# In the first block of a fused attention, MLP and expert kernel: the second weight step of a round placed ahead of two matmul groups, and ScalarE's order left to the planner

## The chip, the cores and the metric

The kernel runs on one core of a Trainium2 chip. The metric is the device time of one execution in microseconds (us). Five engines matter: TensorE (PE), whose weight loads are listed as PEld; VectorE (DVE); ScalarE (ACT); GpSimd (POOL); and SyncE (SP), which only issues transfers. Each runs its own list of instructions in order and waits on semaphores for the others.

## The reference

Everything is float32 at the interface. A chunked attention over 8 batches, 8 heads, 576 positions and a head size of 64 (chunks of 64 positions) is followed by a two-layer MLP and then by a routed layer of 8 experts with a skip.

```
scores = q_c @ k_c^T / 8 ; attn = softmax(scores) ; x = attn @ v_c   # (4608, 512)
h = x @ w_in                       # (4608, 2048)
x = (h * sigmoid(1.702 h)) @ w_out # (4608, 512)
e = argmax(x @ w_gate) ; p = softmax(x @ w_gate)[e]
out = x + p * relu(x @ w1[e]) @ w2[e]   where x @ w_skip > 0, else x
```

The two matrices of the MLP reach the chip as 64-bit floating-point numbers, as pairs of 32-bit words.

## The kernel before

Each large matmul is made of three matmuls on a faster 32-bit format: an operand is split into a high part (`hi`) and what is left (`lo`), and `hi*hi + hi*lo + lo*hi` is summed. The 4608 rows are worked through in nine blocks of 512 (`j`), each in 16 rounds (`i`), one for each 128 of the 2048 hidden columns. A round of the MLP has these steps:

- `emit_h` (lines 289 to 301): 12 matmuls (H) into one of two PSUM banks `hps`; then ACT makes `sg` (tanh, line 299), and DVE makes `sg` final from it and the bank (line 300), which frees the bank.
- `emit_g` (lines 303 to 310): ACT makes `gh` (line 306), DVE makes `gl` (line 309).
- `emit_y` for the round before (lines 312 to 322): 12 matmuls (Y) into four banks `yps`, the first eight from `gh`, the last four from `gl`.

The attention for the next block is made beside it. In the first block, rounds 1, 4, 7, 10 and 13 have a `burst` (lines 216 to 228): PE makes the scores of one tile of 128 positions and the output of the tile before into the same two banks of tag `at`; DVE reduces and subtracts (lines 168 and 170), ACT takes the exponential (line 175) and copies the output out (line 214). Rounds 3, 6, 9, 12 and 15 have `c0` (DVE lines 178 to 181, the softmax's division) and `c1` (PE transposes line 189, ACT copy line 191). Rounds 0, 3, 6, 9 and 12 have `a` (PE transposes of q and k at line 143, ACT copies at line 145). The transposes use the same two `at` banks.

The first block also turns the 64-bit weights into `hi` and `lo` parts, in 33 steps ("ticks"), one for each of the 32 half matrices and one to drain: 8 are done in the prologue and 25 in block 0. A tick is `tick1` then `tick2` (lines 702 to 717). On half `m` DVE does two bit operations (lines 265 and 266) and POOL one add (line 267). On half `m-1` ACT makes the high part (line 276) and DVE the low part (line 277). For half `m+1` ACT reads the raw words (lines 258 and 259), and for half `m+3` SP issues a load of 512 KB (lines 242 and 247). Rounds 0 to 14 each have one tick (called the first tick here), with its `tick1` set between `gh` and `gl`. The ten rounds 0, 1, 3, 4, 6, 7, 9, 10, 12 and 13 have a second one, issued by the `while` loop at lines 799 and 800.

The order of the instructions on each engine is fixed when the program is built. A planner goes through a modelled time line and gives each engine, whenever it is free, the earliest instruction of the program whose inputs and buffers are ready there. Engines named in `tc.manual_schedule` (line 767, open for the 16 rounds of block 0) keep the order of the program instead. Before the change these are ACT, DVE and POOL; PE and SP are the planner's everywhere, and outside block 0 all engines are.

Of the kernel before, what the change touches and what calls it, by code (L numbers as in the profile page):

```python
# [21 lines left out]
def kernel(  # L22
# [14 lines left out]
    PE, ACT, DVE, POOL, SP = nc.tensor, nc.scalar, nc.vector, nc.gpsimd, nc.sync  # L37
# [43 lines left out]
    def bank(shape, tag, name):  # L81
        return pp.tile(shape, F32, tag=tag, name=name, bufs=PB[tag])
# [206 lines left out]
    def emit_h(i, xh, xl):  # L289
        ps = bank([P, BT], "h", "hps")  # L290
        n = 0
        for kk in range(KD):
            wh = whi[i][:, kk * P:(kk + 1) * P]
            wl = wlo[i][:, kk * P:(kk + 1) * P]
            for a, b in ((wh, xh), (wh, xl), (wl, xh)):
                PE.matmul(ps, a, b[:, kk], start=(n == 0), stop=(n == 3 * KD - 1))  # L296
                n += 1
        sg = mp.tile([P, BT], F32, tag="sg", name="sg", bufs=2)
        ACT.activation(out=sg, in_=ps, func=AF.Tanh, scale=0.851)  # L299
        DVE.scalar_tensor_tensor(sg, sg, 1.0, ps, op0=ALU.add, op1=ALU.mult)  # L300
        return sg

    def emit_g(sg, between=None):
        gh = mp.tile([P, BT], F32R, tag="gh", name="gh", bufs=2)
        gl = mp.tile([P, BT], F32R, tag="gl", name="gl", bufs=2)
        ACT.activation(out=gh, in_=sg, func=AF.Copy, scale=0.5)  # L306
        if between is not None:
            between()
        DVE.scalar_tensor_tensor(gl, sg, 0.5, gh.bitcast(F32), op0=ALU.mult, op1=ALU.subtract)  # L309
        return gh, gl  # L310

    def emit_y(i, g, ys):
        gh, gl = g
        wh, wl = whi[i][:, HW:], wlo[i][:, HW:]
        first, last = i == 0, i == NF - 1
        for t in range(TPB):
            cs = slice(t * P, (t + 1) * P)
            PE.matmul(ys[t], gh[:, cs], wh, start=first, stop=False)  # L318
            PE.matmul(ys[t], gh[:, cs], wl, start=False, stop=False)  # L319
        for t in range(TPB):  # L320
            cs = slice(t * P, (t + 1) * P)
            PE.matmul(ys[t], gl[:, cs], wh, start=False, stop=last)  # L322
# [13 lines left out]
    def gate_load():  # L336
        SP.dma_start(out=wgT[:, :, 0:NE], in_=w_gate.rearrange("(k p) e -> p k e", p=P))

    def gate_rows():
        ps = bank([P, DM], "at", "wgp")  # L340
        for kk in range(KD):
            PE.transpose(ps[0:NE, kk * P:(kk + 1) * P], wgT[:, kk, 0:NE], ident)
        rows = mp.tile([P, DM], F32, tag="x2", name="wgrows", bufs=4)[0:NE]
        ACT.copy(out=rows, in_=ps[0:NE])
        SP.dma_start(out=wgd, in_=rows)
# [171 lines left out]
    def first_row(s):  # L517
        src = emeta[0:1, 1, s:s + 1] if s < NFIRST else meta[0:1, 0, s - NFIRST:s - NFIRST + 1]
        return SP.value_load(src, min_val=0, max_val=NROW - SL)
# [14 lines left out]
    def load_next():  # L534
        if cnt["load"] < len(wq):
            s, n, w = wq[cnt["load"]]
            cnt["load"] += 1
            single = s >= NFIRST + NPAIR and w == 0
            raw2.append((s, n, w, None if single else load_w2(expert(s), n, w)))
# [109 lines left out]
    def new_x1():  # L649
        return [mp.tile([P, 2, BT], F32, tag="x1", name="x1", bufs=2) for _ in range(2)]  # L650
# [43 lines left out]
    tick_n = [0]  # L694

    def tick():


        tick1()
        tick2()  # L700

    def tick1():
        m = tick_n[0]
        if m == 0:
            halves[0].s0()
        if m < 2 * NF:
            halves[m].s1()

    def tick2():
        m = tick_n[0]  # L710
        tick_n[0] += 1
        if 1 <= m <= 2 * NF:
            halves[m - 1].s3()
        if m + 1 < 2 * NF:
            halves[m + 1].s0()
        if m + 3 < 2 * NF:
            halves[m + 3].load()

    def ticks_by(i):

        return min(2 * NF + 1, NTICK0 - (-(2 * NF + 1 - NTICK0) * (i + 1) // (NF - 1)))
# [31 lines left out]
    for j in range(NB):  # L753
        lastb = j + 1 == NB
        if not lastb:
            x1 = new_x1()
        else:
            rs.close()
            rawp = rs.enter_context(tc.tile_pool(name="raw", bufs=2, side="right", reuse_waits="tile"))
            for _ in range(4):  # L760
                load_next()
        ys = [bank([P, DM], "y", "yps") for _ in range(TPB)]
        prev = None
        inorder = ExitStack()
        if j == 0:
            assert tick_n[0] == NTICK0
            inorder.enter_context(tc.manual_schedule(engines={ACT.engine, DVE.engine, POOL.engine}))
        for i in range(NF):
            R = j * NF + i
            nc_ = round_of.get(R - 2)  # L770
            if nc_ is not None and nc_ < NST:
                St[nc_].c0()
            sg = emit_h(i, xh, xl)
            span = NF // 2 - 2 if lastb else NF - 5
            nfill = -(-len(fill) // (span - i)) if i < span else 0
            if nfill:
                fill.pop(0)()
                nfill -= 1
            mid = None
            if j == 0:  # L780
                if i == 7:
                    gate_load()
                elif i == 11:
                    gate_rows()
                if tick_n[0] < ticks_by(i):
                    mid = tick1
            g = emit_g(sg, mid)
            if mid is not None:
                tick2()
            if prev is not None:  # L790
                emit_y(i - 1, prev, ys)
            na = round_of.get(R + 1)
            if na is not None and na < NST:
                St[na].a()
                if na + 1 < NST:
                    St[na + 1].load_qk()
            if nc_ is not None and nc_ < NST:
                St[nc_].c1()
            while j == 0 and tick_n[0] < ticks_by(i):
                tick()  # L800
            kb = round_of.get(R)
            if kb is not None:
                if kb:
                    St[kb - 1].x1 = x1
                burst(St[kb] if kb < NST else None, St[kb - 1] if kb else None)
                if kb < NST:
                    St[kb].load_v()
            for _ in range(nfill):
                fill.pop(0)()
            if late and (i >= span or late[0][0] < j):  # L810
                late.pop(0)[1]()
            if lastb:
                if prev is not None:
                    conv_next2()
                if i == NF // 2:
                    gstack.close()
                    m2 = ctx.enter_context(tc.tile_pool(name="m2", bufs=1, reuse_waits="tile"))
                    for s in range(NEARLY):
                        slots[s].list(first_row(s))
                if i >= NF // 2 + 2 and i - NF // 2 - 2 < NEARLY:  # L820
                    slots[i - NF // 2 - 2].gather((NB - 1) * BT)
            prev = g
        inorder.close()
        if j == 0:
            assert tick_n[0] == 2 * NF + 1
            fstack.close()
            gstack = ExitStack()
            gp = gstack.enter_context(tc.tile_pool(name="gates", bufs=1, reuse_waits="tile"))
            wg = gp.tile([P, NE, DM], F32, name="wg")
            ws = gp.tile([P, DM], F32, name="ws")  # L830
            SP.dma_start(out=ws, in_=w_skip.rearrange("(o d) -> o d", o=1).to_broadcast([P, DM]))
            SP.dma_start(
                out=wg, in_=wgd[0:NE].rearrange("(o e) d -> o e d", o=1).to_broadcast([P, NE, DM]))
        if not lastb:
            xhn = split_x1(x1)
            emit_y(NF - 1, prev, ys)
            xh, xl = xhn
        else:
            slots[0].trans()
            emit_y(NF - 1, prev, ys)  # L840
            conv_next2()
        xs = evac_y(j, ys)
        lg = new_lg()
        if not lastb:
            fill = [lambda t=t, e=e, lg=lg, xs=xs: dot(lg, xs, t, e) for t in range(TPB) for e in range(NE + 1)]
            rt = route(j, lg)
            if j == NB - 3:
                rt.insert(3, order)
            late += [(j + 1, f) for f in rt]
# [108 lines left out]
```

## Time and profile before

| | us |
|---|---|
| median of three runs (lowest to highest) | 1240.87 (1239.23 to 1242.0) |
| the profiled execution | 1239.68 |
| span of its trace | 1237.8 |
| PE busy in the span | 1185.6 (96%) |
| DVE busy | 787.3 (64%) |
| ACT busy | 488.5 (39%) |
| POOL busy | 146.6 (12%) |

The span is what the trace covers. Block 0 lies between about 45 and 175 us of it; before that is the prologue, after it come blocks 1 to 8 and the expert stage. In rows of a timeline, brackets hold the time for which the engine stood idle just before the instruction, and what ended it.

### The profile page before, as it was taken

How to read it: one execution, taken by the hardware profiler on the slowest of the kernel's cores; microseconds unless marked ns; L12 is line 12 of the kernel's file. 1: busy time of each engine (PE TensorE's matmuls, PEld its weight loads, DVE VectorE, ACT ScalarE, POOL GpSimd, SP SyncE). 2: the span in 40 equal slices, each digit the busy share in tenths (PEclk: the TensorE clock that was granted, in tenths of full speed). 3: DMA queues.
4: the chain of work that ended last, by engine and by line, in shares of the span. 5: the costliest groups of instructions: out<-in, count | busy, mean ns of one | idle time of the engine just before them, and what ended most of it. 6: DMA issues, size and time to landing. Idle time of an engine off the chain costs nothing. (4 is left out here: it accounts for less than half of the span.)

```text
span 1237.8 us, 20861 instructions
## 1 busy us (share of the span) xinstructions
PE 1185.6 (96%) x7984; PEld 993.1 (80%) x7984; DVE 787.3 (64%) x1771; ACT 488.5 (39%) x825; POOL 146.6 (12%) x137
## 2 busy tenths in 40 slices
PE   6788899999999999999999999999999999999995
PEld 4666678888888888888888888888788989999985
DVE  5778779349548647746926934954885686666421
ACT  5655643333333324334333333332344444444320
POOL 2332310010010000001001001001021022231110
PEclk9999999999999999999999999999999999999998
DMA  9545441122113113113113112301444667666540
GB/s 217 162 145 145 129 162 43 26 55 87 31 33 104 30 32 95 38 37 99 27 43 100 29 27 54 89 14 38 152 143 130 217 173 259 225 229 219 187 137 8
DMA packets 181846, 128.99 MB, mean 104 GB/s; under 512 B 122335, under 2 KB 155359, under 8 KB 181616
## 3 DMA queue, kind: packets, MB, share of 16 engines
q1 hardware_dynamic: 177072, 117.09, 32.8%
q0 software_dynamic: 4672, 10.54, 2.5%
q8 instruction: 64, 1.05, 0.4%
q14 instruction: 38, 0.31, 0.1%
HBM read 103.59 MB, written 25.04 MB: 104 GB/s over the span
## 5 line engine op out<-in xcount | busy, mean ns | idle before, releaser
L296 PE MATMUL hps<-xh,whi 128*128 128x512 f32 x576 | 232.2, 405 | 9.0 <-DVE sg L300 8.0
L318 PE MATMUL yps<-whi,gh 128*128 128x512 f32 x576 | 228.9, 397 | 4.2 <-ACT gh L306 4.2
L296 PE MATMUL hps<-xl,whi 128*128 128x512 f32 x576 | 227.6, 395 | 0.0
L296 PE MATMUL hps<-xh,wlo 128*128 128x512 f32 x576 | 227.1, 394 | 0.5 <-DVE wlo L277 0.5
L319 PE MATMUL yps<-wlo,gh 128*128 128x512 f32 x576 | 225.7, 392 | 0.0
L300 DVE SCALAR_TENSOR_TENSOR sg<-sg,hps 128x512 f32<-128x512 f32 x144 | 98.5, 684 | 181.6 <-ACT sg L299 180.6
L355 DVE CUSTOM_DVE_ANT_0 junk<-x,wg 128x512 f32<-128x512 f32 x256 | 175.8, 687 | 4.0
L545 DVE TENSOR_TENSOR elo<-rawe,ehi 128x1024 fp32r<-128x1024 f32 x88 | 107.4, 1223 | 84.5 <-ACT ehi L544 79.6
L322 PE MATMUL yps<-whi,gl 128*128 128x512 f32 x576 | 155.4, 391 | 0.0
L299 ACT ACTIVATE sg<-hps 128x512 f32<-128x512 f32 x144 | 85.8, 597 | 165.5 <-PE hps L296 165.3
L544 ACT CAST ehi<-rawe 128x1024 fp32r<-128x1024 f32 x88 | 92.3, 1049 | 139.0 <-PE h2p L610 68.1
L306 ACT ACTIVATE gh<-sg 128x512 fp32r<-128x512 f32 x144 | 91.1, 633 | 129.6 <-DVE sg L300 109.7
L296 PEld LDWEIGHTS hps<-xh,whi 128*128 128x128 f32 x576 | 108.7, 190 | 34.0 <-DVE sg L300 10.6
L318 PEld LDWEIGHTS yps<-whi,gh 128*128 128x128 f32 x576 | 108.7, 189 | 28.3 <-ACT gh L306 5.1
L296 PEld LDWEIGHTS hps<-xh,wlo 128*128 128x128 f32 x576 | 108.9, 189 | 23.7 <-DVE wlo L277 0.9
L319 PEld LDWEIGHTS yps<-wlo,gh 128*128 128x128 f32 x576 | 108.8, 189 | 22.0
L296 PEld LDWEIGHTS hps<-xl,whi 128*128 128x128 f32 x576 | 109.0, 189 | 20.9 <-DVE xl L286 0.6
L322 PEld LDWEIGHTS yps<-whi,gl 128*128 128x128 f32 x576 | 107.6, 188 | 22.3
L408 POOL DMA_INDIRECT tab<-pr,pos x36 | 39.6, 1099 | 674.0 <-DVE st L168 336.0
L309 DVE SCALAR_TENSOR_TENSOR gl<-sg,gh 128x512 fp32r<-128x512 f32 x144 | 99.1, 688 | 30.4 <-ACT gh L306 20.3
L610 PE MATMUL h2p<-xT,ehi 128*128 128x256 f32 x640 | 117.2, 283 | 0.0
L610 PEld LDWEIGHTS h2p<-xT,ehi 128*128 128x128 f32 x640 | 102.0, 191 | 2.6
(172 smaller groups left out, 1522.9 us busy)
## 6 DMA issues: line engine op xcount, KB each, us to landing
rawe<-in_moe_w_dram SPq DMA_DIRECT2D x88, 512.0 KB
v<-in_v_dram SPq DMA_DIRECT2D x144, 64.0 KB
x2d<-x SPq DMA_DIRECT2D x36, 256.0 KB
out_dram<-x SPq DMA_DIRECT2D x36, 256.0 KB
q<-in_q_dram SPq DMA_DIRECT2D x32, 256.0 KB
k<-in_k_dram SPq DMA_DIRECT2D x32, 256.0 KB
raw<-in_moe_w_in_dram SPq DMA_DIRECT2D x16, 512.0 KB
raw<-in_moe_w_out_dram SPq DMA_DIRECT2D x16, 512.0 KB
```

Source lines behind the costliest of these rows:

```text
L296: PE.matmul(ps, a, b[:, kk], start=(n == 0), stop=(n == 3 * KD - 1))
L299: ACT.activation(out=sg, in_=ps, func=AF.Tanh, scale=0.851)
L300: DVE.scalar_tensor_tensor(sg, sg, 1.0, ps, op0=ALU.add, op1=ALU.mult)
L306: ACT.activation(out=gh, in_=sg, func=AF.Copy, scale=0.5)
L309: DVE.scalar_tensor_tensor(gl, sg, 0.5, gh.bitcast(F32), op0=ALU.mult, op1=ALU.subtract)
L318: PE.matmul(ys[t], gh[:, cs], wh, start=first, stop=False)
L319: PE.matmul(ys[t], gh[:, cs], wl, start=False, stop=False)
L322: PE.matmul(ys[t], gl[:, cs], wh, start=False, stop=last)
L355: DVE.tensor_tensor_reduce(junk, xs[t], wg[:, e, :] if e < NE else ws, 1.0, 0.0, ALU.mult, ALU.add, lg[:, t, e:e + 1])
L544: ACT.copy(out=hi, in_=raw)
L545: DVE.tensor_tensor(lo, raw, hi.bitcast(F32), op=ALU.subtract)
L610: PE.matmul(ps[:, f], a[:, c], self.xT[:, b, kk], start=(m == 0), stop=(m == 3 * KD - 1))
```

## The change

Two edits. The loop that issues a round's second tick stood behind `emit_y`, `a` (with the load of the next q and k) and `c1`; it now stands right behind the first tick, ahead of `emit_y`. And ACT is taken out of the set whose order is that of the program in block 0; DVE and POOL stay in it.

```diff
-            inorder.enter_context(tc.manual_schedule(engines={ACT.engine, DVE.engine, POOL.engine}))
+            inorder.enter_context(tc.manual_schedule(engines={DVE.engine, POOL.engine}))
...
             if mid is not None:
                 tick2()
+            while j == 0 and tick_n[0] < ticks_by(i):
+                tick()
             if prev is not None:
                 emit_y(i - 1, prev, ys)
...
             if nc_ is not None and nc_ < NST:
                 St[nc_].c1()
-            while j == 0 and tick_n[0] < ticks_by(i):
-                tick()
             kb = round_of.get(R)
```

## Rows read from the trace of the kernel before

**Rows 1.** By stretch: busy PE, PEld, DVE, ACT, POOL; granted clock, transfer share, GB/s.

```profile
45.00:175.00 130.00, 112.44 (x746) 88.51 (x747) 97.42 (x155) 77.78 (x146) 37.92 (x25) 0.97 0.46 136
175.00:300.00 125.00, 125.00 (x867) 102.40 (x866) 85.42 (x226) 42.49 (x79) 4.21 (x5) 1.00 0.23 64
```

**Rows 2.** Waits of TensorE from 45 to 173 us: total, times, longest.

```profile
PE hps L296 <- DVE sg L300: 6.1, 6, 1.6
PE yps L318 <- ACT gh L306: 4.2, 2, 2.3
PE qTp L143 <- ACT x L214: 3.2, 2, 1.6
PE sv L209 <- ACT qT L191: 2.7, 4, 0.7
PE hps L296 <- ACT xh L285: 1.0, 1, 1.0
PE hps L296 <- DVE wlo L277: 0.5, 1, 0.5
```

**Rows 3.** The same view from 175 us to the end.

```profile
PE xTp L589 <- DMA xg<-x2d,gi: 2.8, 1, 2.8
PE hps L296 <- DVE sg L300: 1.8, 1, 1.8
```

**Rows 4.** Timeline of TensorE, first matmuls behind waits in block 0.

```profile
53.94 0.50 PE L296 MATMUL hps<-xh,whi 128*128 128x512 f32 x1 [0.96 <-DVE sg L300]
...
83.88 0.50 PE L296 MATMUL hps<-xh,whi 128*128 128x512 f32 x1 [1.61 <-DVE sg L300]
...
165.51 0.50 PE L318 MATMUL yps<-whi,gh 128*128 128x512 f32 x1 [1.93 <-ACT gh L306]
```

**Rows 5.** Timeline of ScalarE, rounds 3 to 5.

```profile
80.36 0.58 ACT L191 COPY qT<-pTp 128x512 f32<-128x512 f32 x1 [2.98 <-PE pTp L189]
80.84 0.62 ACT L276 CAST whi<-a 128x512 fp32r<-128x512 f32 x1
81.36 0.70 ACT L258 ACTIVATE r<-raw 128x512 f32<-128x512 f32 x1
...
82.51 0.59 ACT L299 ACTIVATE sg<-hps 128x512 f32<-128x512 f32 x1
...
90.28 0.63 ACT L175 ACTIVATE qT<-qT 128x512 f32<-128x512 f32 x1 [1.84 <-DVE qT L170]
90.81 0.63 ACT L214 COPY x<-sv 128x256 f32<-128x256 f32 x2
```

**Rows 6.** Timeline of VectorE, rounds 1 and 3 to 5.

```profile
58.24 0.68 DVE L277 TENSOR_TENSOR wlo<-a,whi 128x512 fp32r<-128x512 f32 x1
...
81.50 0.69 DVE L277 TENSOR_TENSOR wlo<-a,whi 128x512 fp32r<-128x512 f32 x1 [3.00 <-ACT whi L276]
83.13 0.69 DVE L300 SCALAR_TENSOR_TENSOR sg<-sg,hps 128x512 f32<-128x512 f32 x1 [0.94 <-ACT sg L299]
...
85.41 1.79 DVE L277 TENSOR_TENSOR wlo<-a,whi 128x512 fp32r<-128x512 f32 x1
...
89.44 0.74 DVE L170 TENSOR_TENSOR qT<-sv,st 128x256 f32<-128x256 f32 x2
91.97 0.69 DVE L300 SCALAR_TENSOR_TENSOR sg<-sg,hps 128x512 f32<-128x512 f32 x1 [1.79 <-ACT sg L299]
```

**Rows 7.** Busy time of three rounds (4 to 6), from one line-300 start to another.

```profile
83.13:107.41 24.28, 20.03 (x148) 15.77 (x148) 18.32 (x29) 14.41 (x27) 7.61 (x5) 1.00 0.50 141
```

**Rows 8.** The stretch of block 0 with the lowest granted clock, by engine.

```profile
118.00:121.00 3.00, 3.00 (x9) 2.29 (x9) 2.97 (x4) 1.74 (x4) 1.57 (x1) 0.54 1.10 282
```

**Rows 9.** Timeline of GpSimd, its adds in rounds 1 and 4.

```profile
58.50 1.58 POOL L267 TENSOR_TENSOR a<-a,lf 128x512 uint32<-128x512 uint32 x1 [1.78 <-DVE a L266]
...
85.06 1.59 POOL L267 TENSOR_TENSOR a<-a,lf 128x512 uint32<-128x512 uint32 x1 [5.11 <-ACT whi L276]
```

**Rows 10.** Waits of SyncE's queue from 45 to 173 us, the loads of raw weights.

```profile
SPq L247 <- DVE a L266: 36.6, 11, 10.3
```

## The prediction

> **What bounds the kernel now.** I read the busy times by stretch first. From 175 us on, TensorE is busy in every microsecond of the stretch shown (125.00 of 125.00), and in block 0 only 112.44 of 130.00 [rows 1]. Next its waits. From 175 us to the end there are two, 4.6 us together [rows 3]; in block 0 the six kinds listed come to 6.1 + 4.2 + 3.2 + 2.7 + 1.0 + 0.5 = 17.7 us [rows 2]. So the last block and the expert stage are bound by TensorE, and time taken out of block 0 reaches the end undiminished, because nothing behind it waits for a fixed moment. The change can win little more than these 17.7 us, plus what the clock costs: the granted clock of block 0 is 0.97 over 130 us [rows 1], so 0.03 x 130 = 3.9 us at most, lowest at 0.54 from 118 to 121 us, where TensorE ran almost wholly at the lower level of 1.2 GHz [rows 8].
>
> Then, who is late in block 0? Three rounds take 24.28 us, with TensorE busy 20.03, VectorE 18.32, ScalarE 14.41 and GpSimd 7.61 [rows 7]. None is full. VectorE's list shows why: in that period it stands 3.00 us before the low part of the second tick, 0.94 and 1.79 us before line 300, each time for ScalarE [rows 6]. And ScalarE, which has the most room of the three, was itself standing: 2.98 us before the `c1` copy, for transposes that TensorE had put behind other work, and 1.84 us before the exponential, for VectorE's subtraction [rows 5]. In both places instructions whose inputs had long been there stood behind it in the order of the program: the second tick's line 276 and the next `sg` at 80.84 and 82.51 us, the output copies at 90.81. TensorE feels this two steps later, at 83.88 us for instance [rows 4], because only the finished `sg` frees one of its two `hps` banks.
>
> **The change part by part.** *The moved step.* It issues, for each of ten second ticks, three instructions on ScalarE, three on VectorE, one on GpSimd and mostly one load on SP. It passes `emit_y` (TensorE alone), `a` (TensorE and ScalarE), the loads of q and k (SP) and `c1` (TensorE and ScalarE). No instruction of VectorE or GpSimd is passed, so their lists, which stay in program order, stay as they are. On SP the raw load goes ahead of q and k in the program; that queue stood 36.6 us in eleven waits before raw loads until VectorE's line 266 had freed a buffer [rows 10], so the load leaves when VectorE lets it, a little earlier than now. I put it at 0; it could cost a late q and k, but the waits of TensorE in block 0 show no transfer among them [rows 2], and q and k are fetched a burst ahead. On ScalarE the three instructions leave from behind the two copies of `a` and the `c1` copy. They take 82.51 - 80.84 = 1.67 us [rows 5].
>
> *A wait that the move adds.* The second tick's line 276 needs GpSimd's add of the first tick, 1.58 us [rows 9]. In between ScalarE has the first tick's two reads of raw words, 82.51 - 81.36 = 1.15 us by the same pair [rows 5]. So it may wait some 0.4 us, with two reads and the copies of `a` queued behind. Ten times 0.4 us on an engine that has 24.28 - 14.41 = 9.9 us free in three rounds: 0, and 4 us if all of it were on the path.
>
> *ScalarE's free order.* The planner gives ScalarE the earliest instruction whose inputs are there, so the next `sg` need not stand behind `c1`, nor the output copies and the next `sg` behind the exponential. The trace of before has no such order in block 0; the nearest rows are from 175 to 300 us, where ScalarE is the planner's and TensorE never waits, though with ScalarE at 42.49 of 125 us against 77.78 of 130 [rows 1].
>
> I go through TensorE's waits by place.
> - *Behind `c1`.* The waits on line 300 are 6.1 us in six; 0.96 us is the start of the block, 1.61 us that at 83.88 and another like it a period later. With the larger wait for `gh`, 4.2 - 1.93 = 2.3 us, and the 0.5 us for `wlo` that is 2 x 1.61 + 2.3 + 0.5 = 6.0 us [rows 2, 4]. If `sg` goes ahead of the copy, ScalarE starts it up to 2.98 us earlier, more than any of these: all 6.0 go.
> - *Behind the burst.* The other three waits on line 300, 6.1 - 0.96 - 3.22 = 1.9 us, the wait for `gh` at 165.51, 1.9 us, and the two for the output copies, 3.2 us, make 7.0 us [rows 2, 4]. Line 300 can then follow VectorE's subtraction at once, which saves its 1.79 us wait [rows 6]. But the two `at` banks are also held until the subtractions end, at 89.44 + 0.74 = 90.18 us against 90.81 + 0.63 = 91.44 for the copies [rows 5, 6]: of each 1.6 us wait only 1.26 goes and 0.3 stays, 0.7 together. So 6.3 go.
> - *Kept.* The 0.96 us and 1.0 us at the start, where nothing is reordered, and the four waits for the `c1` copy itself, 2.7 us [rows 2].
>
> That is 12.3 us. Against it: a free ScalarE will often have started a read of raw words just before `sg` or `gh` becomes ready. One takes 0.57 us (half of the 1.15), on average half of it is in the way, and with ten waits in play that is 10 x 0.29 = 2.9 us. What is late next is VectorE's list, which without its 5.7 us of waits needs 18.5 of the 20 us that TensorE needs. The sum is 12.3 - 2.9 = 9.4 us. The profiled execution took 1239.68 us (span 1237.8 and 1.9 around it), so 1230.3; the median shown is 1.2 us above that execution, and I name its equivalent, **1231.5 us**. I take nothing for the clock: rounds 4 to 6 hold waits as long as elsewhere and were granted 1.00 throughout [rows 4, 7], so waits alone do not bring it down, and fewer of them may not hold it.
>
> *A rule weighed.* The low-part subtraction took 1.79 us when it began at 85.41, inside GpSimd's add that had begun at 85.06, and 0.68 us when it began at 58.24, ahead of the add at 58.50 [rows 6, 9]. The Trainium skill, SBUF — State Buffer, "Who interferes with whom", says that a VectorE instruction with two SBUF inputs and a GpSimd one that reads SBUF contend for a port pair and that whichever starts first keeps it throughout; by that rule the trace agrees, and it speaks against the move, which brings the second subtraction back beside an add. By the round-1 row the subtraction comes first and the sum stays; the other outcome is the third rival.
>
> **The rivals.**
> 1. *Only the move acts.* The planner may lay ScalarE's `c1` copy and burst where they were. Then just the 1.67 us ahead of `sg` go: 2 x 1.61 + 1.67 + 0.5 = 5.4 us, 1234.3 in the profile, 1235.5 as a median. For it: the planner's own list for TensorE put the transposes of `c1` late. Against it: `sg`'s matmuls were done long before.
> 2. *All of it.* Copies of `a` made early free the `at` banks, `c1` comes ahead of its need, and with dense work the clock holds: 17.7 - 2.0 + 3.9 = 19.6 us, 1221.3 as a median. Against it: VectorE's 18.5 of 20 us leave little room for jitter.
> 3. *The subtraction comes second.* If the high part is late by 0.3 us in rounds 3, 6, 9 and 12, four subtractions begin inside the add, 4 x (1.79 - 0.69) = 4.4 us, all of it on VectorE's path: 9.4 - 4.4 = 5.0 us gained, 1235.9.
> 4. *Slower: reads of raw words taken first.* Raw words and their buffers are ready early, so the planner's list may put both reads ahead of `sg` or `gh`, and VectorE, whose order is fixed, then stands with line 300 or 309 at the head of its queue, the tick's bit operations and the burst behind it. 1.15 us in each of 16 rounds is 18.4 us against the 12.3 won: 6.1 us slower, 1247.0. It decides from the eleventh such round (12.3 / 1.15 = 10.7). For it: VectorE has only 1.5 us to spare in 20, and the planner's modelled times need not be the chip's. Against it: `sg` and `gh` come earlier in the program than the reads that compete.
>
> **How the numbers follow.** Forecast 0.34, only the move 0.14, all of it 0.13, the subtraction 0.07: faster by over 0.2% 0.68. Waits that come back elsewhere to within 0.2% (2.5 us, about what a measurement of this kernel can tell from no change): 0.08. Slower 0.24. The likeliest case's own range is 1227 to 1236, its gain half lost or half as large again. The range runs from the second rival, 1221, to just past the fourth, 1248; about 0.08 lies outside at the top and 0.04 below.
>
> **What would show it.** Right: the lists of VectorE and GpSimd unchanged in block 0; VectorE's 3.00 us wait before line 277 and its 1.79 us before line 300 gone; `sg` on ScalarE ahead of the `c1` copy and of the exponential; TensorE's waits in block 0 near 9 us; three rounds in about 22 us. The first rival shows as a `c1` copy still followed by `sg`; the third as second subtractions of 1.79 us in rounds 3, 6, 9 and 12; the fourth as line 258 and 259 directly ahead of `sg` or `gh`, with VectorE waiting for ScalarE over 1 us in most rounds. The prediction is wrong if block 0 is not shorter, or if what it wins is lost behind 175 us.

## The result, and the profile after

The changed kernel takes 1230.54 us (four runs, 1228.8 to 1230.99) against 1241.02 for the kernel before: a ratio of 0.9913, 95% interval 0.9901 to 0.9925, 10.5 us less. The forecast was 1231.5. The span fell from 1237.8 to 1227.1 us. The terms of the sum were forecast less well than its size.

Busy time by stretch (columns as in [rows 1]), with two stretches of three rounds, 4 to 6 and 7 to 9, from one start of line 300 to another, that answer to [rows 7]:

```profile
45.00:175.00 130.00, 118.06 (x771) 92.64 (x772) 101.09 (x168) 80.95 (x149) 37.66 (x25) 0.97 0.49 147
...
80.44:101.46 21.02, 19.47 (x148) 15.18 (x147) 17.62 (x30) 15.40 (x28) 8.83 (x6) 1.00 0.59 166
101.46:127.02 25.56, 22.68 (x216) 17.90 (x215) 18.38 (x29) 16.08 (x30) 7.77 (x6) 0.93 0.51 153
```

Rounds 4 to 6 now take 21.0 us for 24.3. Rounds 7 to 9 take 25.6, as before (107.41 to 133.01). From line 300 of round 1 to that of round 15 it is 99.9 us for 111.1, of which TensorE stood 7.8 us for 16.1. But round 1 itself comes 2.0 us later, at 61.32 for 59.33, and some of TensorE's work now stands behind line 300 of round 15 instead of ahead of it. A fairer mark is line 300 of round 13 in block 1, at 253.80 us before and at 245.85 after: TensorE has run 1592 matmuls by then in both (first row before, second row after), and the distance stays at 7.9 us up to 860 us.

```profile
0.00:253.80 253.80, 218.91 (x1592) 174.15 (x1593) 177.55 (x347) 129.15 (x240) 50.27 (x45) 0.99 0.47 127
0.00:245.85 245.85, 217.29 (x1592) 172.86 (x1593) 175.65 (x346) 129.94 (x240) 50.35 (x45) 0.99 0.49 131
...
1203.00:1206.00 3.00, 3.00 (x15) 2.91 (x14) 0.00 (x0) 0.00 (x0) 0.98 (x1) 0.50 0.17 66
```

So 7.9 of the 10.7 us come from the prologue and block 0. The other 2.8 come near the end, in the expert stage: 1.3 is a shorter wait for gathered rows, and most of the rest a fall of TensorE's granted clock that only this trace of before has there (the third row; the changed kernel's trace has 1.00 from 1190 to 1214 us).

TensorE's waits, 45 to 163 us, then from 163 us on (they answer to [rows 2, 3]):

```profile
PE qTp L143 <- ACT x L214: 4.2, 2, 2.9
PE hps L296 <- ACT xh L285: 3.8, 1, 3.8
PE wgp L342 <- ACT x L214: 1.7, 1, 1.7
PE hps L296 <- DVE sg L300: 1.0, 1, 1.0
PE yps L318 <- ACT gh L306: 0.8, 2, 0.6
PE qTp L143 <- DVE qT L170: 0.8, 1, 0.8
PE kTp L143 <- ACT x L214: 0.2, 1, 0.2
...
PE hps L296 <- DVE sg L300: 1.8, 1, 1.8
PE xTp L589 <- DMA xg<-x2d,gi: 1.5, 2, 1.1
```

All that stood behind `c1` is gone, and the wait for the `c1` copy with it. Two things grew: the wait at the start (line 285), and the waits for the output copies (line 214), 6.1 us for 3.2. ScalarE's list shows where both come from: the end of the prologue, and round 7's burst. The last two rows are VectorE and TensorE behind it.

```profile
45.63 0.62 ACT L276 CAST whi<-a 128x512 fp32r<-128x512 f32 x1 [2.17 <-POOL a L267]
...
47.26 0.36 ACT L214 COPY x<-pv 128x256 f32<-128x256 f32 x1
...
108.53 0.62 ACT L276 CAST whi<-a 128x512 fp32r<-128x512 f32 x1 [1.32 <-POOL a L267]
...
110.85 0.66 ACT L258 ACTIVATE r<-raw 128x512 f32<-128x512 f32 x1 [1.14 <-DMA raw<-in_moe_w_in_dram]
111.41 0.58 ACT L299 ACTIVATE sg<-hps 128x512 f32<-128x512 f32 x1
111.89 0.37 ACT L214 COPY x<-sv 128x256 f32<-128x256 f32 x1
...
112.03 0.69 DVE L300 SCALAR_TENSOR_TENSOR sg<-sg,hps 128x512 f32<-128x512 f32 x1 [3.36 <-ACT sg L299]
112.31 0.66 PE L143 MATMUL qTp<-ident,q 128*128 128x128 f32 x4 [2.88 <-ACT x L214]
```

In the first stretch a tick of block 0 stands ahead of the last output copy of the prologue and waits 2.17 us for GpSimd; `xh`, the input of the first H, can only follow that copy. In the second, `sg` and the output copy follow a high part that waits for GpSimd and a read that waits for a transfer issued 4.0 us before it landed. VectorE waits 3.36 us for that `sg`, TensorE 2.88 us for the copy. In sum, from 45 to 163 us (the last row is the kernel before):

```profile
ACT whi L276 <- POOL a L267: 25.2, 18, 2.2
ACT r L258 <- DMA raw<-in_moe_w_in_dram: 6.1, 8, 1.3
ACT r L258 <- DMA raw<-in_moe_w_out_dram: 2.1, 4, 1.1
...
ACT whi L276 <- POOL a L267: 2.7, 5, 0.6
```

Before, the first of these was 2.7 us in five waits and the others did not occur. The list is fixed when the program is built, by modelled times. By the planner's rule an instruction is placed when its inputs are there in the model, so in the model the adds and the loads must have been done earlier than they are on the chip. This is inferred from the list; no trace shows the modelled times.

### The profile page after: what moved, and what is told of

Read it like the earlier page. It is cut to its first block, busy times and chain, and to the rows that moved or that the text cites. A ratio compares the mean times of both kernels' runs of the same rounds, so it can differ in the third digit from the quotient of the medians.

```text
span 1227.1 us, 20859 instructions
## 1 busy us (share of the span) xinstructions
PE 1182.5 (96%) x7984; PEld 990.3 (81%) x7984; DVE 785.2 (64%) x1771; ACT 489.1 (40%) x825; POOL 148.0 (12%) x137
## 5 line engine op out<-in xcount | busy, mean ns | idle before, releaser
L309 DVE SCALAR_TENSOR_TENSOR gl<-sg,gh 128x512 fp32r<-128x512 f32 x144 | 101.9, 708 | 35.6 <-ACT gh L306 25.2
```

## The experiments

Each was timed several times (4 to 12 runs) against the kernel before, on the same chip; ratios are to that. "Theory" and "rival" with a letter are those of the expectation shown.

**One half of the change at a time.** The move alone:

```diff
-            inorder.enter_context(tc.manual_schedule(engines={DVE.engine, POOL.engine}))
+            inorder.enter_context(tc.manual_schedule(engines={ACT.engine, DVE.engine, POOL.engine}))
```

> The step moved, ScalarE still in program order in block 0. Theory A (the freed ScalarE makes the gain): only the 1.67 us of the second tick's three ScalarE instructions leave from ahead of sg in the rounds with c1, so about 5.4 us are won, 1235.5 us; ScalarE still waits 2 to 3 us at the c1 copy and 1.8 us at the exponential, and TensorE still waits 1.6 us for the output copies. Rival B (the move makes the gain): 1230.5 us, as the changed kernel, with the c1 wait on ScalarE gone.

Measured: 1238.43 us, ratio 0.9985 (0.9974 to 0.9996), 1.9 us won. The `c1` wait on ScalarE halves, 5.5 us for 11.2, but TensorE's waits barely do:

```profile
PE yps L318 <- ACT gh L306: 3.4, 4, 1.9
PE hps L296 <- DVE sg L300: 3.3, 5, 1.2
PE qTp L143 <- ACT x L214: 3.2, 2, 1.6
PE sv L209 <- ACT qT L191: 2.7, 4, 0.7
PE hps L296 <- DVE wlo L277: 1.7, 2, 0.8
PE wgp L342 <- ACT x L214: 1.0, 1, 1.0
```

By [rows 2], the wait for line 300 lost 2.8 us and that for `gh` 0.8, the one for `wlo` gained 1.2, and one of 1.0 us for an output copy came before line 342. Theory A's direction, at a third of its size; rival B falls. The freed engine alone, with the step where it was:

```diff
-            inorder.enter_context(tc.manual_schedule(engines={ACT.engine, DVE.engine, POOL.engine}))
+            inorder.enter_context(tc.manual_schedule(engines={DVE.engine, POOL.engine}))
```

> ScalarE freed, the step left where it was. Theory A: TensorE's and ScalarE's lists come out as in the changed kernel up to buffer names, since the planner takes ScalarE's ready instructions wherever they stand, so 1230.5 us within 2.5. Rival B (the move makes the gain): near the kernel before, over 1236 us, with the second tick's high part behind the c1 copy again.

Measured: 1229.7 us, 0.9915 (0.9900 to 0.9930). The instruction lists of all five engines are those of the changed kernel, up to the numbers of buffers. So the whole gain is ScalarE's free order, and beside it the moved step does nothing, as theory A has it.

**The late start.** ScalarE in program order for round 0, free from round 1:

```diff
+            if j == 0 and i == 1:
+                inorder.close()
+                inorder.enter_context(tc.manual_schedule(engines={DVE.engine, POOL.engine}))
```

> The changed kernel with ScalarE kept in program order for round 0 alone and freed from round 1 on. Theory A: the high part of half 7 no longer stands ahead of the last output copy of the prologue, so the first H starts at about 45.5 us again instead of 48.2, and 2.7 us are won: 1227.8 us. Rival C (the late start is absorbed, since ScalarE has the same work to do either way and the first rounds wait for it later): the first H is early, but block 0 is as much longer, 1230.5 us.

Measured: 1226.03 us, 0.9880 (0.9863 to 0.9898), about 4 us under the changed kernel. The first H starts at 44.76 us for 48.19, 3.4 us earlier. By its time this is theory A, and rival C's 1230.5 us falls. But the rows do not show that the head start itself was kept: line 300 of rounds 3, 4 and 5 starts at 74.93, 80.56 and 88.03 us, no earlier than in the changed kernel (74.82, 80.44 and 87.90). The gain appears from round 7 on, and line 300 of round 8 comes at 107.68 us for 112.03. There ScalarE's list is another one: this `sg` stands ahead of the high part and the read that it stood behind in the changed kernel.

```profile
105.97 0.59 ACT L299 ACTIVATE sg<-hps 128x512 f32<-128x512 f32 x1
...
107.61 0.62 ACT L276 CAST whi<-a 128x512 fp32r<-128x512 f32 x1 [1.05 <-POOL a L267]
```

The edit also ends and reopens the fixed order between rounds 0 and 1, and VectorE took line 300 of round 1 early, at 54.64 us for 61.32. What the late start alone costs is therefore not shown.

**The reads of raw words.**

```diff
+    hold = [mp.tile([P, DM], F32, tag="x2", name="hold", bufs=4) for _ in range(2)]
+    for t_ in hold:
+        POOL.memset(t_[:, 0:1], 0.0)
...
+            if j == 0 and i == NF - 2:
+                for t_ in hold:
+                    DVE.tensor_copy(out=t_[:, 1:2], in_=t_[:, 0:1])
```

> The changed kernel with two of the four buffers that the reads of raw words (line 258) write held back in block 0, so that such a read can run at most one tick ahead of its use. Theory A: in the changed kernel ScalarE stands 8.2 us in twelve waits at line 258 for raw words that have not landed, with sg and the output copies behind; held back, these waits go, and with them most of TensorE's 2.9 and 1.7 us before transposes: 4 us won, 1226.5 us. Rival D (those waits are slack on ScalarE): 1230.5 us. Rival E (the reads come late for VectorE's bit operations): VectorE waits at line 265, slower than 1232 us.

Measured: 1228.92 us, 0.9909 (0.9895 to 0.9923), no different from the changed kernel. Theory A's 4 us did not come. But the cause was hardly taken away: ScalarE still waits 5.2 us for raw words and 2.8 us for the buffers, 8.0 us for 8.2, and the wait for GpSimd stays the largest:

```profile
ACT whi L276 <- POOL a L267: 18.8, 17, 2.7
...
ACT r L258 <- DMA raw<-in_moe_w_in_dram: 4.2, 4, 1.2
ACT r L258 <- DVE a L266: 2.8, 7, 0.4
```

So the run does not decide how much the reads cost, nor between theory A and rival D.

**A better order in place of freedom.** If the prediction named the right instructions behind the right waits, putting those first by hand should do it, with ScalarE in program order. The next round's H and tanh are issued ahead of `emit_y` (line 300 stays in its round), and the step is moved:

```diff
-            sg = emit_h(i, xh, xl)
+            sg = emit_s(*(early or emit_h(i, xh, xl)))
+            early = None
...
+            if j == 0 and i + 1 < NF:
+                early = emit_h(i + 1, xh, xl)
             if prev is not None:
                 emit_y(i - 1, prev, ys)
```

> ScalarE in program order in block 0, the step moved, and the next round's H matmuls and its tanh (line 299) issued ahead of emit_y, a, c1 and the burst, so that no sg stands behind the c1 copy or the exponential. If what held block 0 was which instructions stood behind these two waits (theory A), most of the 6.0 us behind c1 and the 3.8 us of line 300 and gh behind the burst go without any freedom for the planner on ScalarE: 1231 us; the waits for the output copies (3.2 us) and the c1 copy (2.7 us) stay. Rival F (VectorE's list is the limit): line 300 waits elsewhere, 1236 us or more.

Measured: 1220.39 us, 0.9837 (0.9822 to 0.9851): 20 us won, twice what the freed engine gives and twice what was expected: the waits for the output copies and half of those for the `c1` copy went as well, 4.7 us of 17.9 are left, and the granted clock of block 0 reads 1.00. Rival F falls. Then the output copies ahead of the exponential as well:

```diff
             nxt.b_mm(sc)
+        early_x = old is not None and old.t < 2 * TPB
+        if early_x:
+            old.d_post(pv)
+        if nxt is not None:
             nxt.b_post(sc)
-        if old is not None:
+        if old is not None and not early_x:
             old.d_post(pv)
```

> As the run before it, and in the bursts of block 0 the two output copies issued ahead of the exponential. Theory A: of each 1.6 us wait for them 1.26 goes, 2.5 us less than that run: 1228.5 us, better than the changed kernel because the start is not late. Rival F: no further gain.

Measured: 1219.91 us, 0.9829 (0.9815 to 0.9842), the fastest, though not told apart from the run before it: theory A's 2.5 us did not come, since with `sg` early the wait for the output copies is already gone. TensorE's waits from 45 to 163 us, all of them, and the stretch of [rows 1]:

```profile
PE sv L209 <- ACT qT L191: 1.3, 2, 0.7
PE hps L300 <- ACT xh L289: 1.0, 1, 1.0
PE hps L300 <- DVE sg L307: 1.0, 1, 1.0
PE yps L325 <- ACT gh L313: 0.6, 1, 0.6
PE hps L300 <- DVE xl L290: 0.5, 1, 0.5
PE kTp L143 <- ACT wgrows L351: 0.2, 1, 0.2
...
45.00:175.00 130.00, 126.21 (x888) 100.84 (x888) 112.53 (x201) 82.45 (x156) 37.35 (x25) 1.00 0.52 155
```

4.6 us are left of 17.9, and the granted clock of the stretch is 1.00. On ScalarE `sg` now precedes the copies, and nothing waits long in front of it (line numbers are shifted here: 303 is the tanh, 280 the high part; 307 and 313 above are lines 300 and 306):

```profile
75.37 0.62 ACT L280 CAST whi<-a 128x512 fp32r<-128x512 f32 x1 [0.48 <-POOL a L271]
...
77.06 0.57 ACT L303 ACTIVATE sg<-hps 128x512 f32<-128x512 f32 x1
...
78.84 0.59 ACT L191 COPY qT<-pTp 128x512 f32<-128x512 f32 x1 [0.27 <-PE pTp L189]
```

**The output copies by themselves.** The second edit above, alone, on the kernel before:

> The kernel before with one edit: in the bursts of block 0 the two output copies are issued ahead of the exponential on ScalarE. By the term of the prediction the two 1.6 us waits before the transposes shrink to 0.3 us: 2.5 us won, 1238.4 us. Rival G (the transposes then wait as long for the banks, which VectorE's subtractions hold, or line 300 comes no earlier so the matmuls behind wait instead): no change, 1240.9 us.

Measured: 1235.34 us, 0.9952 (0.9938 to 0.9965), 5.9 us won, over twice the term. The two 1.6 us waits are gone wholly, while the waits for line 300 and `gh` stay (304 and 310 here):

```profile
PE hps L300 <- DVE sg L304: 5.3, 4, 1.6
PE yps L322 <- ACT gh L310: 4.3, 3, 2.3
```

By its time rival G falls. But the two traces do not put the rest of the gain into block 0. TensorE's waits there are 3.3 us fewer, the granted clock is 0.95 for 0.97 (some 2.6 us of the 130, by an estimate), and the line 300 that stood at 253.80 us comes only 0.75 us earlier, at 253.05. The traces differ by 4.2 us, most of it near the end, where the wait for gathered rows is 1.4 us shorter and the fall of the clock at 1203 us is missing. So what the output copies cost by themselves stays open.

In the freed kernel with the early start, the copies moved to VectorE, ahead of its reductions:

```diff
+        if early_x:
+            old.d_post(pv, DVE.tensor_copy)
```

> The kernel of e3_start (1226.0 us) with the output copies of block 0's bursts moved from ScalarE to VectorE, ahead of its reductions. Theory H (the output copies are late in the freed kernels because they stand on ScalarE behind waits for GpSimd's add and for raw words): the 3.1 + 0.3 us of TensorE's waits for them fall to about 1 us: 1223.5 us. Rival F (VectorE has no room): two copies of 0.36 us more in each of four bursts push line 300 back by 0.7 us each: 1226 us or slower.

Measured: 1223.8 us, 0.9856 (0.9841 to 0.9871). That is 2 us or so under the start experiment; the two were timed on different occasions and their intervals overlap. TensorE's waits for the copies are gone, those for `gh` grow from 1.6 to 4.1 us. Theory H and the rival both hold in part.

**Is freedom worth anything beside a good order?** The fastest kernel, with ScalarE freed:

```diff
-            inorder.enter_context(tc.manual_schedule(engines={ACT.engine, DVE.engine, POOL.engine}))
+            inorder.enter_context(tc.manual_schedule(engines={DVE.engine, POOL.engine}))
```

> The kernel of k6_hand (1219.9 us) with ScalarE taken out of the program order in block 0, so it differs from it by the freed engine alone. Theory A (the freedom is a rough substitute for a good order: the planner goes by a modelled time line in which GpSimd's add and the raw loads are done earlier than on the chip): the start is late again and ScalarE stands before line 276 for GpSimd and before line 258 for raw words, about 1228 us. Rival J (freedom adds to a good order): 1220 us or less.

Measured: 1232.24 us, 0.9923 (0.9910 to 0.9937): 12 us lost by that one line. Theory A, at more than its price; rival J falls. ScalarE's waits for GpSimd and for raw words (280 and 262 here) are back, as is the late start:

```profile
ACT whi L280 <- POOL a L271: 25.0, 17, 2.3
ACT r L262 <- DMA raw<-in_moe_w_in_dram: 6.6, 8, 1.5
...
PE hps L300 <- ACT xh L289: 5.3, 2, 3.8
```

And the move, in the hand order: the kernel with `sg` early, its second tick back behind `c1`.

> The kernel of k7_sg_early (1220.4 us) without the move: the second tick back behind emit_y, a and c1, ScalarE in program order. Theory K (with sg out of the way, the second tick's high part is the last thing left behind the c1 copy, and VectorE's low part and line 300 wait for it in rounds 3, 6, 9 and 12): 0.9 us in each, 1224 us. Rival L (the move is worth nothing in any order, as with the freed engine): 1220.4 us.

Measured: 1228.09 us, 0.9895 (0.9880 to 0.9910), 7 us more than with the move, twice theory K's price; rival L falls. VectorE waits where theory K says, 11.0 us in four, for the high parts behind `c1`:

```profile
DVE wlo L277 <- ACT whi L276: 11.0, 4, 3.7
```

So the same move is worth 0 with ScalarE free, 1.9 us alone and about 7 us with `sg` out of the way.

## Why the prediction was right, and where it was not

*What bounds block 0.* Right, and the hand order shows it best: TensorE was held by instructions standing on ScalarE behind two waits that were not theirs. Taking these out of the way, with VectorE's order in block 0 unchanged, won 21 us.

*The moved step at 0.* Right in the changed kernel, shown by identical lists. VectorE's and GpSimd's lists of block 0 are those of before, as said.

*Behind `c1`, 6.0 us.* Gone as forecast: line 300 from 6.1 to 1.0 us (the 0.96 at the start), `gh` from 4.2 to 0.8, `wlo` from 0.5 to 0. Rounds 4 to 6 took 21.0 us where about 22 was named, though rounds 7 to 9 still took 25.6. The way was not wholly the one described. `sg` went ahead of the `c1` copy in rounds 3 and 12; in rounds 6 and 9 the copy still comes first (at 100.36 us, `sg` at 100.83), but it no longer waits, since its transposes are done long before (at 95.69). That is a part of the second rival.

*Kept.* Wrong on both counts. The four waits for the `c1` copy, 2.7 us, went too: the planner now copies q and k early (in round 3 at 71.83 us for 76.32) and makes the transposes before they are needed (at 75.09 us, for matmuls at 81.24). And "the start, where nothing is reordered" was reordered: a freed engine takes an instruction of block 0 into the prologue when the model calls it ready. That cost 2.8 us in the wait, and round 1 came 2.0 us later.

*Behind the burst, output copies from 3.2 to 0.7 us.* Wrong: 6.1 us. The term took it that a freed ScalarE runs a copy as soon as its input is there on the chip; it runs it where the model put it. Line 300's wait of 1.79 us, which was to go, is gone in round 5, but it is 3.36 us in round 8 and 1.55 in round 11.

*Reads started just before, 2.9 us.* The right place, but another mechanism and mis-sized: not an instruction of 0.57 us in the way, but waits for GpSimd and for transfers, 33.4 us on ScalarE. The wait for GpSimd's add had been named, at 0.4 us ten times, and put at 0; it measured 25.2 us in 18 waits. This is the fourth rival's mechanism at less than its price: a read that waited for its transfer stands directly ahead of `sg` at 80.46 and at 110.85 us, not in most rounds.

*The sum.* It put 9.4 us into block 0. TensorE's waits there fell from 17.9 to 12.5 us, by 5.4, and not to near 9. Up to the mark at 253.80 us the gain is 7.9: these 5.4, 0.9 in the prologue, and 1.6 us less busy time of TensorE (217.29 for 218.91), which I have not broken down. The last 2.8 us came near the end, where the sum had nothing, from the gather wait and a fall of the clock that is there in one trace and not in the other. Terms of both signs cancelled, so the nearness of 1230.5 to 1231.5 is luck.

*The clock at 0.* Right in these two traces: 0.97 over the stretch both before and after, with two falls in each. The prediction names only the one at 118 us, and its "waits as long as elsewhere" leaves out the longest, 2.28 us at 134.41, behind which the second fall came. But the freed engine alone, with the same lists, has one fall and 0.99, so the clock of one trace is not that of the kernel.

*The subtraction beside the add.* The second subtractions of rounds 3 and 6 took 0.68 us (79.84 and 99.63), so the third rival did not come there. By the rule of the Trainium skill weighed in the prediction (SBUF — State Buffer, "Who interferes with whom") the trace agrees: each began ahead of its add (80.10 and 99.89).

*The first rival's price.* 5.4 us was forecast for the move alone and 1.9 measured: 1.67 us less ahead of `sg` did not become 1.67 us less for TensorE. Line 300 and `gh` gave 3.6 us, but 2.7 came back before other matmuls, 1.2 of it for `wlo` and 1.0 for an output copy.

## What to carry to other kernels

When an engine with room stands at the head of its queue, list what stands behind it with its inputs ready, and put the one whose result frees the busiest engine first: here one early `sg` and one moved step were worth 20 us. Freeing such an engine to a planner can find half of that and hide the rest, because the planner orders by modelled times; look then for long waits on engines that never waited before, and for work pulled across the edge of the freed stretch. An edit that does nothing in one order may be worth 7 us in another, so try it again after the order changes.

## What was not expected of the hardware

The granted clock did not follow TensorE's waits in a simple way. Before, it fell twice in block 0: at 118 us [rows 8], and again behind the wait of 2.28 us that ended at 134.41. In the changed kernel it fell behind the two longest waits inside block 0, of 2.88 us, ended at 112.31, and of 1.74 us, ended at 135.90. A mean of 0.65 means that it ran at the lower level of 1.2 GHz for most of the stretch. The rows are before, the changed kernel twice, and the freed engine alone:

```profile
135.00:138.00 3.00, 3.00 (x9) 2.37 (x8) 2.97 (x4) 2.51 (x5) 1.50 (x1) 0.53 0.71 188
...
112.00:115.00 3.00, 2.69 (x10) 2.15 (x11) 2.94 (x5) 1.58 (x4) 1.05 (x1) 0.65 0.05 15
137.00:140.00 3.00, 3.00 (x9) 2.20 (x8) 3.00 (x4) 1.03 (x3) 1.56 (x1) 0.50 0.37 107
...
137.00:140.00 3.00, 2.91 (x14) 2.21 (x14) 2.97 (x4) 1.02 (x2) 1.58 (x1) 1.00 0.26 61
```

The last row stands behind the same wait (1.73 us, ended at 136.26) in the same order of instructions, and there the clock did not fall. With the buffers held back it stayed at 1.00 from 54 to 175 us in spite of waits of 1.9 and 1.8 us. In the hand order, whose longest wait of TensorE in block 0 is 1.0 us, it did not fall either, and by an estimate 0.03 x 130 = 3.9 us of clock came back at most. Which wait brings the clock down, these runs do not show.

The 1.00 shown for the very start of block 0 does not fit the pace there. Before, matmuls of line 296 started 0.43 us apart at 47.13 us and 0.23 us apart at 50.10, with the granted clock shown as 1.00 at both. In the trace of the move alone it is 0.50 from 45 to 48 us.

VectorE's line 309 took 1.78 us instead of 0.69 when it began beside an add of GpSimd (120.08 and 120.02 us), as the subtraction of line 277 does [rows 6, 9].
